# The tile of the rests moved to second to last, and the last unit's stores joined: linear attention feeding a four-expert mixture on one core

## The chip, the core and the metric

The kernel runs on one core of a Trainium2 chip. The core has a matrix engine (TensorE; PE for its matmuls and PEld for its weight loads in the profile), a vector engine (VectorE, DVE), a scalar engine (ScalarE, ACT), a general engine (GpSimd, POOL) and a queue engine (SyncE, SP), and 16 DMA engines that all queues share. Each engine works through its own instructions strictly in the order in which they were emitted, and waits for the others through semaphores. The metric is the device time of one launch in microseconds; lower is better.

## What is computed

```python
# q, k, v: (8 batches, 8 heads, 576 rows, 64); N = 8*576 = 4608, D = 512, E = 4, F = 1024
phi = lambda x: where(x > 0, x, exp(x) - 1) + 1
kv  = einsum('bhsd,bhse->bhde', phi(k), v)                       # 64 x 64 for each head
z   = phi(k).sum(over rows)
x   = (phi(q) @ kv) / (phi(q) . z + 1e-6)                        # attention, per head
x   = x.transpose(0, 2, 1, 3).reshape(4608, 512)                 # one row per token
p   = domain_probs / (domain_probs.sum(-1) + 1e-9)
out = sum over e of p[:, e] * (relu(x @ w1[e]) @ w2[e])          # w1: 512x1024, w2: 1024x512
```

Every batch has 576 tokens: 512 that make a full tile, and a rest of 64.

## The kernel before, in words

**Tiles and units.** The expert part works on nine tiles of 512 tokens. Tiles 0 to 7 are the first 512 tokens of each batch. Tile 8 collects the rests of all eight batches, 8 x 64 tokens; its input is the tensor `xT_left`. A *unit* is one tile with one expert. Each unit has a first layer of two blocks (class `Block`, matmuls of L868, steps p1 to p7 with c22, into the PSUM banks `b` and `e`) and a second layer of 14 products (`layer2_product`, matmuls of L810, into the bank `py`). Both layers use a seven-product scheme of 2 x 2 blocks (Strassen-Winograd), for which GpSimd forms the sums of hidden blocks (`hidden_sum`, L777 to L783) and of tokens (`token_sum`, L849). The output of a tile is kept in four SBUF tiles `acc` (128 tokens x 512 each). For expert 0 ScalarE writes them first (L704), afterwards VectorE adds to them (L706). `acc` has five buffers, so that a new tile's `acc` waits for stores of the tile before.

**Attention ahead of the experts.** While the units of tile j run, the attention of batch j+1 is worked out in between (`batch_steps`). For the full tile of a batch SP issues a transposing DMA of phi(q) (`dma_qT`, L393), PE multiplies (`nd`, L472), VectorE divides, and SP issues four transposing DMAs into `xT` (`dma_xT`, L524). The rest of a batch goes a similar way in smaller pieces: `load_left` (L297) loads k, v and q of the 64 rows as two DMAs each, one for each half of the heads; `left_act` and `left_dve` (L375 to L386) make phi(q) in `qlp`; `dma_qTl` (L401) turns it by two transposing DMAs into `qz`; `nd_left` (L490) is four small matmuls that read `qz`, two VectorE instructions, and two transposing DMAs (L504) into `xT_left`. `qz` is one buffer for all batches. The rest of batch 0 is only begun late: in `before` its q is loaded and turned while tile 7 runs.

**The order of work** is a list. Every step is put at a position, the list is sorted by position, and each engine's instructions are emitted in that order; a step that issues on several engines takes its place on each of them. One unit takes 14 positions, one tile 56. Position 0 of a *window* is the first step of its tile's first unit; window j is that of tile j (units of tile j are `2 * NSLOT * n` positions after `base`). A block that starts at position s has p1 at s, p2 at s+3, p6 at s+5, p7 at s+8, p5 at s+9, p4 at s+11 and p3 at s+13; a unit's second layer starts 20 positions after the unit, at the offsets `L2AT`. `ATTN[1]` holds the positions of a batch's attention within a window, `LATE` those of batch 0's rest. The first part of the kernel, up to the start of tile 2, follows a list written out by hand (`EARLY`); the change does not touch it.

**The end.** The very last unit (tile 8, expert 3) uses another order of products (1, 2, 5, 6, 7, 3, 4), and each quarter of the output (128 tokens x 256 columns) is stored as soon as it is complete. `store` (L693) sends it as two DMAs of 64 KB, one for each batch whose rests lie in it, on two of the queues of SP, ACT and POOL:

```python
by = {(7, 0): "PP", (7, 1): "PA"}.get((p, i), "SA")
store(j, ns, ds, [on[x] for x in by])
```

The full tiles are stored by one DMA of 256 KB for each 128 tokens (L687, SP).

Of the kernel before, what the change touches and what calls it, by code (L numbers as in the profile page):

```python
# [11 lines left out]
FP32 = mybir.dt.float32  # L12
# [18 lines left out]
            v=(18.1, 19.16, 22.55, 30.55),  # L31
            k=(-5.5, 26.3, 27.5, 28.5),
            kd=(0.5, 27.07, 30.0, 30.7),
            lv=23.45,
            lk=15.35,
            lkd=16.3,
            kv=34.0,
            q=(36.4, 36.95, 40.2, 43.4),
            qd=(37.75, 39.0, 40.55, 44.7),
            lq=54.05,  # L40
            lqd=54.5,
            qt=(42.1, 45.0, 45.8, 46.25),
            nd=(46.7, 47.0, 47.05, 47.8),
            xt=(48.15, 50.45, 51.45, 54.8),
            qtl=57.23,
            nl=71.0,
# [4 lines left out]
            v=(4.4, 8.7, 12.1, 14.8),  # L51
            k=(0.3, 2.9, 6.7, 11.25),
            kd=(7.1, 3.84, 14.3, 14.8),
            lv=10.36,
            lk=9.9,
            lkd=11.6,
            kv=19.1,
            q=(20.1, 22.1, 27.0, 30.0),
            qd=(21.75, 27.2, 30.2, 32.3),
            lq=33.9,  # L60
            lqd=38.3,
            qT=35.9,
            nd=(39.3, 40.4, 42.0, 43.5, 45.3, 46.1),
            nl=52.1,
        ),
    ),
    "HSUM": ((-5.2, -3.9, -3.7, -1.3), (0.3, 2.7, 2.7, 5.7)),
    "L2ORD": (2, 5, 1, 6, 3, 7, 4),
# [1 line left out]
    "TSUM": (-6.7, -4.7, -1.6, -0.7),  # L70
    "TSUM1": (3.76, 4.1, 6.3, 9.92),
    "PR": (-21.88, 47.0, 56.27, 39.85),
    "LATE": (4.0, 14.0, 16.0, 24.0),
    "LQ": 'SSSA',
    "LK": 'ASSS',
    "LV": 'SSSS',
# [4 lines left out]
    "KC": ('AA', 'AV', 'VA', 'AA'),  # L81
    "XT": ('AA', 'AA', 'AV', 'AV'),
    "CUT": (((0, 2, 4),) * 4, ((0, 2, 4),) * 4),
    "MOVE": {"m83.10": 512.0, "m83.11": 512.0, "m83.20": 512.0, "m83.21": 512.0, "m82.41": 528.0},
    "WARM": (14, 3, 2, 1, 5),
    "BANK": {'qT0': 'py', 'qT1': 'b', 'nd00': 'py', 'nd00+': 'b', 'kv2': 'py', 'xT00': 'b', 'kv3': 'b', 'nd10+': 'b', 'L00': 'b', 'L10': 'py', 'nd01': 'b', 'xT01': 'py', 'nd11+': 'b', 'L20': 'e', 'L30': 'e', 'L01': 'e', 'L11': 'py', 'L21': 'py', 'L31': 'b', 'b1.qT3': 'py', 'b1.nd30': 'py', 'b1.nd21': 'b', 'b1.q1': 'b', 'b1.qT1': 'py', 'b1.nd01': 'py', 'b1.xT2': 'b', 'b1.nd11': 'py', 'b1.xT0': 'b'},
    "EARLY": (
# [36 lines left out]
def kernel(  # L124
# [10 lines left out]
    nc = tc.nc  # L135
    ATTN, HSUM, L2ORD, L2AT = (CFG[x] for x in ("ATTN", "HSUM", "L2ORD", "L2AT"))

    B, H, S, D = q.shape
    N, E = moe_domain_probs.shape
    _, Dm, F = moe_w1.shape  # L140

    P = 128
    HP = P // 2
# [12 lines left out]
    NACC = 5  # L156
# [3 lines left out]
    NH = NT // 2  # L160
    FH = FC // 2
    DH = Dm // 2
    SE = (0, 1, 2, 3)
    BIG = 3.0e38
    ENG = mybir.EngineType

# [112 lines left out]
    class Batch:  # L279
# [5 lines left out]
            self.vl = vl  # L285

        def alloc_left(self):
            self.rl = praw.tile([P, 3, HG, D], FP32, tag="rawl", bufs=1, name="rl")

        def load_left(self, *names, eng=nc.sync, us=(0, 1)):  # L290
            b = self.b
            if self.rl is None:
                self.alloc_left()
            for i, (name, src) in enumerate((("k", k), ("v", v), ("q", q))):
                for u in us:
                    if name in names:
                        eng.dma_start(  # L297
                            out=self.rl[u * HP : (u + 1) * HP, i],
                            in_=src[b, u * HG : (u + 1) * HG, SM:S].rearrange(
                                "h r d -> r h d"  # L300
                            ),
                        )
# [59 lines left out]
        def left_act(self, *names):  # L362

            for name in names:
                i = ("k", "v", "q").index(name)
                src = self.rl[:, i].rearrange("p h d -> p (h d)")
                parts = []
                for u in range(2) if name == "k" else ():
                    us = slice(u * HP, (u + 1) * HP)
                    parts.append((us, self.kl[us, 2 * u : 2 * u + 2].rearrange("p a d -> p (a d)")))  # L370
                if name == "q":
                    self.ql = pa.tile([P, HG, D], FP16, tag="qlp", bufs=1, name="qlp")
                    parts.append((slice(0, P), self.ql.rearrange("p h d -> p (h d)")))
                for us, dst in parts:
                    nc.scalar.activation(dst, src[us], AF.Identity, bias=1.0)  # L375
                el = aps([P, HG * D], FP32, "psum_el")
                nc.scalar.activation(el, src, AF.Exp)
                self.ph["l" + name] = el, parts
# [302 lines left out]
    def new_py():  # L681
        return ppm.tile([P, Dm], FP32, tag="py", bufs=2, name="py")

    def store(j, ns, cols=slice(0, Dm), engs=(nc.sync, nc.scalar)):
        acc = accs[j, ns][:, cols]
        if j < B:
            nc.sync.dma_start(  # L687
                out=out_b[j, 0:SM].rearrange("(p c) d -> c p d", c=CM)[ns],
                in_=acc,
            )  # L690
        else:
            for u in range(2):
                engs[u].dma_start(  # L693
                    out=out_b[2 * ns + u, SM:S, cols],
                    in_=acc[u * HP : (u + 1) * HP],
                )
# [88 lines left out]
    def layer2_product(j, e, hT, hss, p, i):  # L785


        if (j, e) == (NTILES - 1, E - 1):
            if p == 1:
                pys[j, e, i] = [ppm.tile([P, DH], FP32, tag=tag, bufs=2, name=f"p{tag}") for tag in ("b", "e")]  # L790
            run, side = pys[j, e, i]
        else:
            if p == 2:
                pys[j, e, i] = new_py()
            run, side = pys[j, e, i][:, 0:DH], pys[j, e, i][:, DH:Dm]
        ts = slice(i * P, (i + 1) * P)
        ts2 = slice(NH + i * P, NH + (i + 1) * P)
        w, tw = w2_sb[e], t2_sb[e]
        lo, hi = slice(0, FH), slice(FH, FC)
        ps, lhsT, rhs, first = {  # L800
            1: (run, lambda k: hT[k // 2][:, k % 2, 0, ts], w[:, lo, 0:DH], (j, e) == (NTILES - 1, E - 1)),
            2: (side, lambda k: hT[k // 2][:, k % 2, 1, ts], w[:, hi, 0:DH], True),
            5: (side, lambda k: hss[k // 2][0][:, k % 2, ts], tw[:, 0], True),
            6: (run, lambda k: hss[k // 2][1][:, k % 2, ts], tw[:, 1], False),
            7: (run, lambda k: hT[k // 2][:, k % 2, 0, ts2], w[:, lo, DH:Dm], False),
            3: (side, lambda k: hss[k // 2][3][:, k % 2, ts], w[:, hi, DH:Dm], False),
            4: (run, lambda k: hT[k // 2][:, k % 2, 1, ts2], tw[:, 2], False),
        }[p]
        for k in range(FH):
            nc.tensor.matmul(  # L810
                out=ps,
                lhsT=lhsT(k),
                rhs=rhs[:, k],
                start=first and k == 0,
                stop=k == FH - 1,
                skip_group_check=True,
            )
        yield
        c1, c2 = slice(0, DH), slice(DH, Dm)
        ns, ds, first = {  # L820
            2: (i, c1, True),
            5: (2 + i, c2, True),
            1: (i, c1, False),
            6: (i, c2, True),
            7: (2 + i, c2, False),
            3: (i, c2, False),
            4: (2 + i, c1, True),
        }[p]
        add_acc(j, e, ns, ps, ds, first and e == 0)
        if (j, e) == (NTILES - 1, E - 1):  # L830
            if p in (2, 3, 4, 7):
                yield
                by = {(7, 0): "PP", (7, 1): "PA"}.get((p, i), "SA")
                store(j, ns, ds, [on[x] for x in by])
        elif e == E - 1 and p in (3, 4):
            yield
            store(j, ns)
# [96 lines left out]
    def batch_steps(bt, nxt, put, at, at_next):  # L934
# [50 lines left out]
        else:  # L985
            put(at["qT"], f"b{b}.qT", bt.dma_qT)
            for i in range(6):
                put(at["nd"][i], f"b{b}.nd{i}", numerators, 3 * i, min(3, NPAIR * CM - 3 * i))
        put(at["nl"], f"b{b}.nl", bt.nd_left)
        if first:  # L990
            put(at["xl"], f"b{b}.xl", bt.pe_xl)

# [11 lines left out]
    with tc.manual_schedule(  # L1004
# [53 lines left out]
                put_at(CFG["WS1"][e][i], f"s{e}.{i}", weight_sums, e, i)  # L1058
                put_at(CFG["WS2"][e][i], f"t{e}.{i}", weight_sums2, e, i)
        base = CFG["BLK"][6]  # L1060
        units = [(j, e) for j in range(1, NTILES) for e in range(E)]
        for n, (j, e) in enumerate(units):
            h, hss = [None, None], [[None] * 4, [None] * 4]
            at = base + 2 * NSLOT * n
# [16 lines left out]
        for j in range(0, NTILES - 1):  # L1081
            at = base + 2 * NSLOT * E * (j - 1) if j else 0.0

            def put(pos, *g, at=at):
                put_at(at + pos, *g)

            if j + 1 < B:
                nxt = bts[j + 2] if j + 2 < B else None
                batch_steps(bts[j + 1], nxt, put, ATTN[j > 0], ATTN[1])
            else:  # L1090
                put(CFG["LATE"][0], "b0.alloc", b0.alloc_left)
                put(CFG["LATE"][0], "b0.load", b0.load_left, "q")
                put(CFG["LATE"][1], "b0.lq", b0.left_act, "q")
                put(CFG["LATE"][2], "b0.lqm", b0.left_dve, "q")
                put(CFG["LATE"][2] + 1, "b0.qTl", b0.dma_qTl)
                put(CFG["LATE"][3], "b0.nl", b0.nd_left)
            for i in range(4):
                if j:
                    put(2 * NSLOT * E + CFG["TSUM"][i], f"ts{j + 1}.{i}", token_sum, j + 1, i)
                else:  # L1100
                    put(base + CFG["TSUM1"][i], f"ts1.{i}", token_sum, 1, i)
        work = [(CFG["MOVE"].get(w[2], w[0]), *w[1:]) for w in work]
# [48 lines left out]
```

## Time and profile before

| | |
|---|---|
| runs before, us | 487.11, 487.05, 485.85; median 487.05 |
| span of the profiled execution, first to last instruction, us | 484.6 |
| median of the runs less that span, us | 2.5 |
| PE busy | 474.4 us, 98% of the span |
| DVE, POOL, ACT busy | 377.3, 358.3 and 332.2 us |
| DMA, mean rate over the span | 111 GB/s |

The profile page and the runs do not say which of the three runs the profiled execution is closest to; its span is used beside the median, with the 2.5 us between them kept as they are. In the lines below, a row of the timeline has the start, the length, the engine, the source line, the operation, what it writes and reads, and how many instructions were merged in it. `SPq` and `ACTq` are the queue sides of those engines: the length of a DMA there is the time that the queue takes to issue it, not the time until the data has landed. `L504` is line 504 of the kernel.

### The profile page before, as it was taken

To read this page: it belongs to the slowest core of one execution; us is meant where nothing else is said; L and a number is where in the kernel's file an instruction comes from. 1 tells how busy PE (TensorE), PEld (TensorE's weight loads), DVE (VectorE), ACT (ScalarE), POOL (GpSimd) and SP (SyncE) were. 2 spreads that over 40 slices of the span, in tenths; PEclk is the share of its full clock that TensorE was granted. 3 is DMA by queue.
4 is the path that set the end of the run, shared out by engine and by line. 5 is a ranking of instruction groups with operands and counts; after the bars stand their busy time and mean duration, and the time that the engine had idled before them with its cause. 6 is when DMAs were issued, how large, how long until landed. Compare 5 with 4: busy or idle time off the path is not lost.

```text
span 484.6 us, 12013 instructions
## 1 busy us (share of the span) xinstructions
PE 474.4 (98%) x4565; PEld 407.2 (84%) x4565; DVE 377.3 (78%) x794; ACT 332.2 (69%) x662; POOL 358.3 (74%) x343
## 2 busy tenths in 40 slices
PE   6999999999999999999999999999999999999996
PEld 2766766898889888998889888988898888888885
DVE  5768987987868895888679886988687756775676
ACT  5689989956895599649884888478944565446530
POOL 5566044689966986789777977697769877987775
PEclk9999999999999999999999999999999999999999
DMA  8999987543445154523552446323221020002003
GB/s 293 216 217 254 233 204 201 134 109 88 123 144 111 42 156 150 120 53 115 172 135 56 114 133 157 77 77 106 69 59 28 7 93 2 1 0 89 2 1 87
DMA packets 79945, 53.67 MB, mean 111 GB/s; under 512 B 45152, under 2 KB 72608, under 8 KB 79888
## 3 DMA queue, kind: packets, MB, share of 16 engines
q1 hardware_dynamic: 69760, 40.43, 30.4%
q0 software_dynamic: 8896, 11.47, 12.3%
q10 hardware_dynamic: 1232, 1.02, 0.6%
q8 instruction: 35, 0.57, 0.5%
q14 instruction: 22, 0.18, 0.1%
HBM read 45.16 MB, written 9.44 MB: 113 GB/s over the span
## 4 chain that ended last, share of the span: by engine, by line
PE 90%; DMA 5%; DVE 2%; ACT 2%; issue 0%; POOL 0%; SPq 0%; ACTq 0%; DVEq 0%
PE py L810 38%; PE pb L868 24%; PE pe L868 18%; PE py L715 4%; DMA w<-in_moe_w_dram 2%; PE ph L655 1%; PE psum_nd L472 1%; DMA rawq<-in_q_dram 1%; DMA rawb<-in_q_dram 1%; DMA out_dram<-acc 1%; PE psum_kv L444 1%; PE pb L810 1%; PE pe L810 1%; DVE acc L706 0%; PE psum_nl L490 0%
## 5 line engine op out<-in xcount | busy, mean ns | idle before, releaser
L706 DVE SCALAR_TENSOR_TENSOR acc<-py,p_sb,acc 128x256 f32<-128x256 f32 (+1 forms) x382 | 182.2, 488 | 42.7 <-PE py L810 39.1
L852 DVE CUSTOM_DVE_ANT_0 h<-pe,u 128x512 f16<-128x512 f32 x140 | 96.1, 688 | 45.3 <-PE pe L868 28.0
L868 PEld LDWEIGHTS <-w 128*128 128x128 f16 x1120 | 108.9, 98 | 16.2
L777 POOL TENSOR_TENSOR hs<-h 128x512 f16<-128x512 f16 x64 | 74.7, 1167 | 56.9 <-DVE h L852 51.0
L810 PEld LDWEIGHTS <-h 128*128 128x128 f16 x1024 | 99.6, 98 | 12.2 <-issue 0.9
L810 PE MATMUL py<-w,h 128*128 128x256 f16 x744 | 106.4, 273 | 0.5 <-ACT acc L704 0.5
L879 ACT COPY u<-pb 128x512 f32<-128x512 f32 x140 | 82.4, 591 | 29.7 <-PE pb L868 27.8
L779 POOL TENSOR_TENSOR hs<-hs,h 128x512 f16<-128x512 f16 x64 | 74.1, 1157 | 26.8 <-PE py L810 24.3
L868 PEld LDWEIGHTS <-s 128*128 128x128 f16 x840 | 81.2, 98 | 12.6 <-DVE s L747 0.7
L868 PE MATMUL pb<-tt,w 128*128 128x256 f16 x560 | 83.8, 273 | 0.0
L810 PEld LDWEIGHTS <-hs 128*128 128x128 f16 x768 | 74.4, 98 | 8.8 <-issue 0.2
L783 POOL TENSOR_TENSOR hs<-h,hs 128x512 f16<-128x512 f16 x64 | 74.2, 1159 | 0.8 <-POOL h L781 0.5
L781 POOL TENSOR_TENSOR h<-h 128x512 f16<-128x512 f16 x64 | 74.6, 1165 | 0.1
L810 PE MATMUL py<-t,hs 128*128 128x256 f16 x496 | 74.1, 273 | 0.0
L901 ACT ACTIVATE h<-pe 128x512 f16<-128x512 f32 x70 | 41.9, 599 | 41.1 <-PE pe L868 40.5
L894 ACT COPY pe<-pb 128x512 f32<-128x512 f32 x70 | 40.0, 571 | 41.3 <-PE pb L868 15.8
L922 ACT ACTIVATE h<-pb 128x512 f16<-128x512 f32 x70 | 41.8, 599 | 6.3 <-PE pb L868 6.2
L868 PE MATMUL pb<-tt,s 128*128 128x256 f16 x280 | 41.9, 273 | 0.2 <-DVE s L747 0.2
L868 PE MATMUL pe<-tt,s 128*128 128x256 f16 x280 | 42.0, 273 | 0.0
L868 PE MATMUL pe<-xT,s 128*128 128x256 f16 x248 | 37.1, 273 | 0.0
L868 PE MATMUL pb<-xT,w 128*128 128x256 f16 x248 | 37.1, 273 | 0.0
L868 PE MATMUL pe<-xT,w 128*128 128x256 f16 x248 | 37.0, 273 | 0.0
(133 smaller groups left out, 594.6 us busy)
## 6 DMA issues: line engine op xcount, KB each, us to landing
out_dram<-acc SPq DMA_DIRECT2D x32, 256.0 KB, 2.5
w<-in_moe_w_dram POOLq DMA_DIRECT2D x14, 512.0 KB, 10.6
rawb<-in_k_dram SPq DMA_DIRECT2D x24, 256.0 KB, 3.1
rawb<-in_q_dram SPq DMA_DIRECT2D x24, 256.0 KB, 2.7
rawb<-in_v_dram SPq DMA_DIRECT2D x24, 256.0 KB, 2.8
w<-in_moe_w_dram POOLq DMA_DIRECT2D x4, 256.0 KB, 5.8
rawb<-in_k_dram POOLq DMA_DIRECT2D x4, 256.0 KB, 10.5
rl<-in_q_dram SPq DMA_DIRECT2D x16, 64.0 KB, 3.1
```

The source lines that it names most:

```text
L706: nc.vector.scalar_tensor_tensor(out=acc, in0=ps, scalar=pscal, in1=acc, op0=AO.mult, op1=AO.add)
L777: nc.gpsimd.tensor_tensor(out=hs[0], in0=a21, in1=a22, op=AO.add)
L779: nc.gpsimd.tensor_tensor(out=hs[1], in0=hs[0], in1=a11, op=AO.subtract)
L781: nc.gpsimd.tensor_tensor(out=a21, in0=a11, in1=a21, op=AO.subtract)
L783: nc.gpsimd.tensor_tensor(out=hs[3], in0=a12, in1=hs[1], op=AO.subtract)
L810: nc.tensor.matmul(out=ps, lhsT=lhsT(k), rhs=rhs[:, k], start=first and k == 0, stop=k == FH - 1, skip_group_check=True,)
L852: nc.vector._custom_dve(TENSOR_ADD_SAT, out=out, in0=ps, in1=u, s0=BIG, s1=0.0)
L868: nc.tensor.matmul(out=ps[:, kk], lhsT=lk(kc), rhs=rhs[:, kc], start=first and kk == 0 and kc == 0, stop=kc == 1, skip_group_check=True,)
L879: nc.scalar.copy(u, self.b)
L894: nc.scalar.copy(self.e5, self.b)
L901: nc.scalar.activation(self.h[:, :, 0, 0:NH], self.e5, AF.Relu)
L922: nc.scalar.activation(self.h[:, :, 1, 0:NH], self.b, AF.Relu)
```

## The change

Five things change.

1. **Order of tiles.** Units run over tiles 0 to 6, then 8, then 7 (`TILES`). The last unit is now tile 7 with expert 3 (`LAST`), and the token sums follow the same order.
2. **Stores.** The last unit's quarters go out by one DMA of 128 KB each, on SP for i = 0 and on ACT for i = 1; POOL issues none. Tile 8, now in the middle of the stream, is stored by two DMAs of 128 KB for each 128 tokens, all on SP.
3. **Batch 0's rest** is worked out in window 3 (while tile 3 runs and the attention of batch 4 is made) instead of window 7: its q is loaded at position 36, phi on ACT at 48.6 and on DVE at 50, the two transposing DMAs of L401 at 50.1, and `nd_left` at 55.4. Before, in window 7, these were 4, 14, 16, 17 and 24. Its raw q goes into a buffer of `acc` instead of a buffer of its own.
4. **Batch 4's rest**: `nd_left` moves from position 52.1 to 47.2 of the same window 3.
5. **Batch 7's rest** (window 6): phi(q) from 33.9 (ACT) and 38.3 (DVE) to 23.3 and 24.4, and with it its transposing DMAs from 40.3 to 26.4; `nd_left` from 52.1 to 37.2.

```diff
+        dict(
...
+            lq=23.3,
+            lqd=24.4,
...
+            nl=37.2,
+        ),
...
-    "LATE": (4.0, 14.0, 16.0, 24.0),
+    "LATE": (36.0, 48.6, 50.0, 50.1, 55.4),
...
+    TILES = (*range(B - 1), NTILES - 1, B - 1)
+    LAST = (TILES[-1], E - 1)
...
         def alloc_left(self):
-            self.rl = praw.tile([P, 3, HG, D], FP32, tag="rawl", bufs=1, name="rl")
+            if self.b:
+                self.rl = praw.tile([P, 3, HG, D], FP32, tag="rawl", bufs=1, name="rl")
+            else:
+                self.rl = pm.tile([P, 2, HG, D], FP32, tag="acc", bufs=NACC, name="rl")
...
-    def store(j, ns, cols=slice(0, Dm), engs=(nc.sync, nc.scalar)):
+    def store(j, ns, cols=slice(0, Dm), eng=nc.sync):
         acc = accs[j, ns][:, cols]
         if j < B:
-            nc.sync.dma_start(
-                out=out_b[j, 0:SM].rearrange("(p c) d -> c p d", c=CM)[ns],
+            eng.dma_start(
+                out=out_b[j, 0:SM].rearrange("(p c) d -> c p d", c=CM)[ns][:, cols],
                 in_=acc,
             )
         else:
             for u in range(2):
-                engs[u].dma_start(
+                eng.dma_start(
                     out=out_b[2 * ns + u, SM:S, cols],
                     in_=acc[u * HP : (u + 1) * HP],
                 )
...
-        if (j, e) == (NTILES - 1, E - 1):
+        if (j, e) == LAST:
             if p in (2, 3, 4, 7):
                 yield
-                by = {(7, 0): "PP", (7, 1): "PA"}.get((p, i), "SA")
-                store(j, ns, ds, [on[x] for x in by])
+                store(j, ns, ds, (nc.sync, nc.scalar)[i])
...
-        put(at["nl"], f"b{b}.nl", bt.nd_left)
+        put(at["nl"] - 4.9 * (b == 4), f"b{b}.nl", bt.nd_left)
...
-        units = [(j, e) for j in range(1, NTILES) for e in range(E)]
+        units = [(j, e) for j in TILES[1:] for e in range(E)]
...
-                batch_steps(bts[j + 1], nxt, put, ATTN[j > 0], ATTN[1])
-            else:
+                batch_steps(bts[j + 1], nxt, put, ATTN[(j > 0) + (nxt is None)], ATTN[1])
+            if j == 3:
                 put(CFG["LATE"][0], "b0.alloc", b0.alloc_left)
                 put(CFG["LATE"][0], "b0.load", b0.load_left, "q")
                 put(CFG["LATE"][1], "b0.lq", b0.left_act, "q")
                 put(CFG["LATE"][2], "b0.lqm", b0.left_dve, "q")
-                put(CFG["LATE"][2] + 1, "b0.qTl", b0.dma_qTl)
-                put(CFG["LATE"][3], "b0.nl", b0.nd_left)
+                put(CFG["LATE"][3], "b0.qTl", b0.dma_qTl)
+                put(CFG["LATE"][4], "b0.nl", b0.nd_left)
...
-                    put(2 * NSLOT * E + CFG["TSUM"][i], f"ts{j + 1}.{i}", token_sum, j + 1, i)
+                    put(2 * NSLOT * E + CFG["TSUM"][i], f"ts{TILES[j + 1]}.{i}", token_sum, TILES[j + 1], i)
```

In the diff, five steps of the last two units that an entry of `MOVE` sets to a fixed position keep their positions under the names of tile 7.

More of the change, by code (lines that the diff above doesn't have):

```diff
@@ L65 @@
         ),
+        dict(
+            v=(4.4, 8.7, 12.1, 14.8),
+            k=(0.3, 2.9, 6.7, 11.25),
+            kd=(7.1, 3.84, 14.3, 14.8),
+            lv=10.36,
+            lk=9.9,
+            lkd=11.6,
+            kv=19.1,
+            q=(20.1, 22.1, 27.0, 30.0),
+            qd=(21.75, 27.2, 30.2, 32.3),
+            lq=23.3,
+            lqd=24.4,
+            qT=35.9,
+            nd=(39.3, 40.4, 42.0, 43.5, 45.3, 46.1),
+            nl=37.2,
+        ),
     ),
@@ L83 @@
     "CUT": (((0, 2, 4),) * 4, ((0, 2, 4),) * 4),
-    "MOVE": {"m83.10": 512.0, "m83.11": 512.0, "m83.20": 512.0, "m83.21": 512.0, "m82.41": 528.0},
+    "MOVE": {"m73.10": 512.0, "m73.11": 512.0, "m73.20": 512.0, "m73.21": 512.0, "m72.41": 528.0},
     "WARM": (14, 3, 2, 1, 5),
@@ L162 @@
     DH = Dm // 2
-    SE = (0, 1, 2, 3)
+    TILES = (*range(B - 1), NTILES - 1, B - 1)
+    LAST = (TILES[-1], E - 1)
     BIG = 3.0e38
@@ L297, in load_left @@
                         eng.dma_start(
-                            out=self.rl[u * HP : (u + 1) * HP, i],
+                            out=self.rl[u * HP : (u + 1) * HP, i if self.b else 0],
                             in_=src[b, u * HG : (u + 1) * HG, SM:S].rearrange(
@@ L365, in left_act @@
                 i = ("k", "v", "q").index(name)
-                src = self.rl[:, i].rearrange("p h d -> p (h d)")
+                src = self.rl[:, i if self.b else 0].rearrange("p h d -> p (h d)")
                 parts = []
@@ L800, in layer2_product @@
         ps, lhsT, rhs, first = {
-            1: (run, lambda k: hT[k // 2][:, k % 2, 0, ts], w[:, lo, 0:DH], (j, e) == (NTILES - 1, E - 1)),
+            1: (run, lambda k: hT[k // 2][:, k % 2, 0, ts], w[:, lo, 0:DH], (j, e) == LAST),
             2: (side, lambda k: hT[k // 2][:, k % 2, 1, ts], w[:, hi, 0:DH], True),
@@ L829, in layer2_product @@
         add_acc(j, e, ns, ps, ds, first and e == 0)
-        if (j, e) == (NTILES - 1, E - 1):
+        if (j, e) == LAST:
             if p in (2, 3, 4, 7):
                 yield
-                by = {(7, 0): "PP", (7, 1): "PA"}.get((p, i), "SA")
-                store(j, ns, ds, [on[x] for x in by])
+                store(j, ns, ds, (nc.sync, nc.scalar)[i])
         elif e == E - 1 and p in (3, 4):
```

## The prediction

> **What bounds the kernel now.** I read the engine totals first, then the busy time of the windows, the timeline of SP, PE and ACT at the places that the change touches, and the last microseconds.
>
> ```profile
> PE 474.4 (98%) x4565; PEld 407.2 (84%) x4565; DVE 377.3 (78%) x794; ACT 332.2 (69%) x662; POOL 358.3 (74%) x343
> 165.80:216.70 50.90, 50.90 (x511) 45.58 (x509) 41.05 (x91) 37.92 (x76) 40.74 (x38) 1.00 0.45 115
> 369.60:418.60 49.00, 49.00 (x453) 43.95 (x452) 33.36 (x68) 26.64 (x50) 40.35 (x37) 1.00 0.09 29
> 467.50:484.60 17.10, 12.52 (x114) 10.82 (x111) 12.46 (x28) 1.18 (x2) 10.67 (x11) 0.94 0.22 61
> ```
>
> The last three rows are windows (start:end, length, then busy time of PE, PEld, DVE, ACT, POOL, granted clock, DMA share, GB/s): window 3, window 7, and the end. In windows 3 and 7 PE is busy for all of their length. So no step that is moved there can win time for the middle of the kernel; a step can only lose time, by making PE wait. What can be won lies behind PE's last matmul (480.0), in the stores. The first part is unchanged, and the work of PE is the same in number.
>
> **The stores at the end.**
>
> ```profile
> 479.62 0.92 DVE L706 SCALAR_TENSOR_TENSOR acc<-pb,p_sb,acc 128x256 f32<-128x256 f32 x2
> 481.42 0.55 ACTq L693 DMA_DIRECT2D out_dram<-acc  x1
> DMA to landing us min/median/max: 2.2/2.2/2.3
> ```
>
> The last data is ready at 479.62 + 0.92 = 480.54, but its second DMA goes out at 481.42, 0.88 us later, since ACT still issues earlier ones at about 0.65 us apart. (The third row is of the last DMA on SP and the last on ACT.) It lands 2.2 us after, at 483.6; from there to the end of the span it is 1.0 us. With one DMA for each quarter, SP and ACT take turns: VectorE finishes a quarter every 0.45 us, so each queue gets one in 0.9 us, more than its 0.55 us. The queue is free, and the last issue follows the data within 0.05 us, at 480.59: **-0.83 us**. The DMA is now 128 KB instead of 64; the 256 KB stores of L687 land in 2.0 us at best and 2.4 in the median, so I take 2.3 instead of 2.2: **-0.75 us** (from -0.5 to -1.0). PE's and VectorE's order in the last unit is the same for tile 7 as for tile 8.
>
> **Batch 0's rest in window 3.** This is where I expect the loss. SP in that window:
>
> ```profile
> 195.78 2.55 SPq L393 DMA_TRANSPOSE qT<-qp  x1
> 198.42 1.29 SPq L297 DMA_DIRECT2D rl<-in_k_dram  x2
> 199.76 1.27 SPq L297 DMA_DIRECT2D rl<-in_v_dram  x2
> 201.07 2.41 SPq L297 DMA_DIRECT2D rl<-in_q_dram  x2
> 203.60 2.47 SPq L401 DMA_TRANSPOSE qz<-qlp  x2
> 206.23 5.13 SPq L524 DMA_TRANSPOSE xT<-x_sb  x4
> 214.74 2.44 SPq L504 DMA_TRANSPOSE xT_left<-x_sl  x2
> ```
>
> From 195.78 to 211.36 SP issues without a break: one transposing DMA costs it 1.2 us, so the queue, not the DMA engines, is full. The pause before 214.74 is the wait for batch 4's `nd_left` (PE at 213.62). By position the changed queue reads: L393 (35.9), **two loads for batch 0 (36)**, six loads (39.3), two L401 (40.3), four L524 (40.4 to 46.1), two L504 of batch 4 (now 47.2), **two L401 of batch 0 (50.1)**, two L504 of batch 0 (55.4).
>
> - The two new loads: such a pair takes 1.27 to 1.29 us, the third pair 2.41. Six loads took 5.18, 0.86 each, so two cost 1.3 to 2.4; I take 0.86 x 2 = 1.7. The four L524 then end at 211.36 + 1.7 = 213.06.
> - Batch 4's L504 no longer wait for PE, they wait for SP: 213.1 to 215.55 (2.44).
> - Batch 0's first L401 goes out at 215.6, the second 1.29 later (203.60 to 204.89) at 216.9, and lands 2.3 us after, at **219.2**.
>
> PE needs both. What stands there:
>
> ```profile
> 216.03 0.60 PE L868 MATMUL pe<-xT,s 128*128 128x256 f16 x4
> 216.47 0.60 PE L810 MATMUL py<-w,h 128*128 128x256 f16 x4
> 216.91 0.60 PE L868 MATMUL pb<-xT,w 128*128 128x256 f16 x4
> ```
>
> These are positions 55 (p3 of a block at 42), 55.2 (a second-layer product at 48 + 7.2) and 56 (p1 of the next tile). `nd_left` at 55.4 falls between the last two, so it is due at 216.9. PE is in order: everything behind it waits to 219.2, **+2.3 us**. With loads of 1.3 it is 1.9, with 2.4 it is 3.0; and were the loads to cost nothing, 0.6 would stay. PE has no slack later in which to win it back. The four matmuls themselves are only moved from window 7.
>
> What else belongs to this step: phi(q) is two ACT and one DVE instruction of about 0.45 us each. At 48.6 ACT has a pause of 1.1 us (209.6 to 210.7), and DVE reaches 50 at about 211.5, well ahead of SP: nothing. The buffer of `acc`: four are held by tile 3, the fifth is free, and it is back before tile 4 asks: nothing, or up to 0.3 if the buffers come round in another order and ACT waits for a store, as it does at 293.27, where PE lost 0.2 us. SP's loads for batch 5 come 3 us later at most, behind the two L504 of batch 0, while PE has stood still for 2.3: nothing. GpSimd's token sums for tile 4 need the L524, 1.7 later; the second sum starts at 215.2, the last L524 lands at 214.2: nothing.
>
> **Batch 4 earlier.** `nd_left` at 47.2 comes after the group at 208.82, at 209.26. The second L401 of batch 4 now lands at 207.2 + 1.7 = 208.9. It fits by 0.35 us; with the slowest loads it is late by 0.3, but then the later stall is shorter by that. So 0.
>
> **Batch 7 earlier.** Its phi(q) at 23.3 falls into the busiest stretch of ACT:
>
> ```profile
> 340.35 0.61 ACT L347 ACTIVATE psum_ee<-rawb 128x512 f32<-128x512 f32 x1
> 340.97 0.47 ACT L704 ACTIVATE acc<-py,p_sb 128x256 f32<-128x256 f32 x1
> 342.08 0.60 PE L810 MATMUL py<-t,hs 128*128 128x256 f16 x4
> ```
>
> Two ACT instructions of about 0.43 us come between the first two rows. ACT is without a pause from 338 to 345.6, so the first `acc` ends at 342.3 instead of 341.44, and the PE group of 342.08, which overwrites that half of `py`, waits some 0.3 us: **+0.3** (0 if ACT catches up first, 0.86 at most, what is put in).
>
> **Tile 8 in the middle.** Its stores are eight DMAs on SP instead of four. The third pair ends its issue some 0.65 us later and lands at about 442.4, and ACT's fourth `acc` of the next tile begins at 442.81: 0, at most 0.2.
>
> **The sum.** -0.75 + 2.3 + 0.3 = +1.85 on the span, 484.6 to 486.4. The span lies 2.5 under the median of the runs, which I keep: 487.05 + 1.85 = **488.9 us**. Its own range is 487.8 (-1.0 + 1.9 - 0.15 for small gains in the last unit) to 490.0 (-0.5 + 2.6 + 0.86, loads near their middle).
>
> **Rivals.**
>
> *A: the clock falls in the stall (490.7).* The granted clock drops soon after PE stops:
>
> ```profile
> 482.00:482.50 0.50, 0.00 (x0) 0.00 (x0) 0.00 (x0) 0.00 (x0) 0.00 (x0) 0.99 0.96 303
> 482.50:483.00 0.50, 0.00 (x0) 0.00 (x0) 0.00 (x0) 0.00 (x0) 0.00 (x0) 0.50 0.75 240
> 1.19 4.66 PE L997 MATMUL warm_ps<-qz 128*128 128x512 f16 x13 [1.19 <-DVE qz L176]
> ```
>
> It is at half by 482.5, 2.5 us after the last matmul, and a stall of 2.3 is near that. What half rate costs: the first 13 matmuls of 512 columns take 4.66 us, where at full rate a 256-column one starts every 0.109 us, so 13 of double length would take 2.8. That is 1.8 us lost, hence 488.9 + 1.8 = 490.7. Against it: one stop of the clock at the end is all that the trace shows, and 2.3 is shorter than 2.5. The Trainium skill ("TensorE: Matmul & The Clock Gate", section "What's actually happening") has the clock halved only after a whole free-running window of about 3.4 us without work. By that rule a stall of 2.3 can't halve it, and the sum stays at 488.9. The trace does not quite agree, with its 2.5 us. I give this case 0.13.
>
> *B: the loads hide (487.2).* If the two loads cost SP nothing, because the third pair's 2.41 us was a wait that comes anyway, the second L401 lands at 217.5 and PE loses 0.6. With +0.3 for batch 7 and -0.75 this is +0.15: no change. It decides at SP's shift: with 1.3 us or less the whole change stays under 0.3%. The profile speaks against it, as the other two pairs were issued back to back at 1.3. I give 0.17.
>
> *C: PE does not stall (486.3).* If batch 0's L401 land before 216.9, the end's -0.75 is all that is left: 486.3, not slower. This needs SP to reach position 50.1 by 213.3 instead of 215.6, that is, to issue the eight transposing DMAs ahead of it from 205.3 on at 1.0 us each, gaps included. Those of this window take 1.2 and more, and 1.3 from one to the next. 0.06.
>
> **Chances.** Forecast 0.64, A 0.13, B 0.17, C 0.06. About 0.3% (1.5 us) is what a measurement of this kernel can tell from no change; the three runs of before are 1.3 us apart. Slower by more than that is over 488.5: seven tenths of the forecast and all of A, 0.58. Within: the rest of the forecast, B and C, 0.38. Faster by over 0.3% would need more than the end can give: 0.04. The range of 486.9 to 490.8 leaves out C, the tails of the forecast and part of A.
>
> **What would show it.** In the changed profile: SP back to back from 195.8 to about 218; PE idle of about 2.3 us at 217, put down to L490 and the DMA into `qz`, and none at batch 4's `nd_left`; a gap of PE of 0.3 us near 344.5 at batch 7's phi(q); the last store issued within 0.1 us of the last DVE instruction. The prediction is wrong if PE runs through window 3, or if the clock column falls below 1.00 there.

## The result and the profile after

The changed kernel took **488.41 us** in the median of 7 runs (486.74 to 490.56), beside 487.05 for 7 runs of the kernel before (485.85 to 487.36). The ratio is 1.0046, with a 95% interval of 1.003 to 1.0062: 2.2 us slower by the ratio, 1.4 by the medians. Line numbers are about 20 higher than before: L830 is the second layer, L887 the first, L510 `nd_left`, L421 the transposing DMAs into `qz`, L524 those into `xT_left`, L544 those into `xT`, L317 the loads of a rest, L707 the last unit's stores.

The profiled execution is the slowest of the seven (490.56). Its span is 488.8, 4.2 over that of before, and it holds one loss that not every run has. First the engine totals of the page, then one row of the waits (us in all, times, the longest):

```profile
PE 476.9 (98%) x4565; PEld 408.3 (84%) x4565; DVE 378.6 (77%) x794; ACT 331.6 (68%) x662; POOL 356.3 (73%) x340
```

```profile
PE psum_nl L510 <- DMA qz<-qlp: 2.5, 2, 1.5
```

PE has as many instructions as before (4565) and is busy 2.5 us longer, so its instructions became longer somewhere; and it waits 2.5 us, in two pieces, for the DMAs of L421. The timeline of PE (start, length, engine, line, operation, number merged, idle time before and what ended it) has both:

```profile
216.98 0.60 PE L830 MATMUL py<-w,h 128*128 128x256 f16 x4
219.04 0.23 PE L510 MATMUL psum_nl<-kvz,qz 128*128 128x130 f16 x1 [1.46 <-DMA qz<-qlp]
220.31 0.34 PE L510 MATMUL psum_nl<-kvz,qz 128*128 128x130 f16 x3 [1.03 <-DMA qz<-qlp]
220.49 0.60 PE L887 MATMUL pb<-xT,w 128*128 128x256 f16 x4
```

Ends of matmuls are modelled, so I count from start to start. The group of 216.98 would be followed at 217.42 (four times 0.109). The next block starts at 220.49, and the four small matmuls take 0.23 when nothing holds them up. So 220.49 - 217.42 - 0.23 = **2.84 us** are lost. The same stretch in windows, cut where the granted clock changes (columns as in the prediction):

```profile
217.68:221.09 3.41, 1.01 (x10) 0.82 (x11) 0.95 (x4) 0.00 (x0) 3.41 (x5) 1.00 0.11 22
221.09:224.50 3.41, 3.41 (x18) 2.44 (x17) 1.21 (x3) 3.21 (x6) 0.79 (x1) 0.50 0.11 22
224.50:228.00 3.50, 3.50 (x34) 3.12 (x33) 3.00 (x6) 2.51 (x6) 3.13 (x3) 1.00 0.50 150
```

The stall fills most of the first row and ends at 220.3, but in the second row the clock stands at 0.50: PE is "busy" all of it and gets 18 matmuls done, where the third row has 34. From start to start, the 20 matmuls from 220.93 up to the group of 224.78 take 3.85 us; at 0.109 each they would take 2.18, so another **1.7 us** are lost. SP's side of the window:

```profile
201.71 2.07 SPq L317 DMA_DIRECT2D rl<-in_v_dram  x2
...
207.85 5.12 SPq L544 DMA_TRANSPOSE xT<-x_sb  x4
213.06 3.54 SPq L524 DMA_TRANSPOSE xT_left<-x_sl  x2
216.72 2.44 SPq L421 DMA_TRANSPOSE qz<-qlp  x2
```

The queue is in the order that the prediction wrote down, and back to back from 196.3 to 219.2. Two things differ. Of the four pairs of loads (199.06 to 205.10) only this one, 2.07, is over 1.29: the longer pair comes once, as it did among three before. And the pair of L524 took 3.54, where it had taken 2.44. Last the tail, where the last data is ready at 484.81 + 0.92 = 485.73:

```profile
484.81 0.92 DVE L726 SCALAR_TENSOR_TENSOR acc<-pb,p_sb,acc 128x256 f32<-128x256 f32 x2
...
485.76 0.34 ACTq L707 DMA_DIRECT2D out_dram<-acc  x1
```

The last DMA goes out 0.03 us after its data and lands 1.97 us later. From PE's end to the end of the span it is 3.57 us, against 4.55 before: **-0.98**.

Together: 0.5 by which the unchanged first part happened to run longer (the matmuls of batch 4's `kv` start at 183.63 instead of 183.12), 2.84, 1.7, 0.17 for a longer wait for `acc` at 299 (501 ns from one matmul's start to the next, instead of 335 at 293.79 before), and -0.98. That is 4.2, the whole difference of the spans.

### The profile page after: what moved, and what is told of

Read it like the earlier page. It is cut to its first block, busy times and chain, and to the rows that moved or that the text cites. A ratio compares the mean times of both kernels' runs of the same rounds, so it can differ in the third digit from the quotient of the medians.

```text
span 488.8 us, 12011 instructions
## 1 busy us (share of the span) xinstructions
PE 476.9 (98%) x4565; PEld 408.3 (84%) x4565; DVE 378.6 (77%) x794; ACT 331.6 (68%) x662; POOL 356.3 (73%) x340
## 4 chain that ended last, share of the span: by engine, by line
PE 94%; DMA 2%; DVE 2%; ACT 1%; issue 0%; SPq 0%; ACTq 0%
PE py L830 38%; PE pb L887 25%; PE pe L887 19%; PE py L735 6%; PE ph L675 1%; PE psum_nd L492 1%; PE psum_kv L464 1%; DMA rawq<-in_q_dram 1%; DMA out_dram<-acc 1%; PE pb L830 1%; PE pe L830 1%; DMA qz<-qlp 0%; PE psum_nl L510 0%; DVE acc L726 0%; ACT ee L601 0%; DVE kpos L586 0%
## 5 line engine op out<-in xcount | busy, mean ns | idle before, releaser
L887 PEld LDWEIGHTS <-w 128*128 128x128 f16 x1120 | 109.1, 98 | 16.3
L830 PEld LDWEIGHTS <-h 128*128 128x128 f16 x1024 | 99.7, 98 | 12.6 <-issue 1.2
L830 PE MATMUL py<-w,h 128*128 128x256 f16 x744 | 106.7, 273 | 0.8 <-ACT acc L724 0.8
L887 PEld LDWEIGHTS <-s 128*128 128x128 f16 x840 | 81.5, 98 | 12.3
L887 PE MATMUL pb<-tt,w 128*128 128x256 f16 x560 | 84.3, 274 | 0.0
L830 PEld LDWEIGHTS <-hs 128*128 128x128 f16 x768 | 74.8, 98 | 9.2 <-issue 0.2
L830 PE MATMUL py<-t,hs 128*128 128x256 f16 x496 | 74.7, 274 | 0.0
L887 PE MATMUL pe<-tt,s 128*128 128x256 f16 x280 | 42.5, 275 | 0.0
L887 PE MATMUL pb<-tt,s 128*128 128x256 f16 x280 | 41.8, 273 | 0.0
L887 PE MATMUL pe<-xT,s 128*128 128x256 f16 x248 | 37.1, 273 | 0.0
L887 PE MATMUL pb<-xT,w 128*128 128x256 f16 x248 | 37.1, 273 | 0.0
L887 PE MATMUL pe<-xT,w 128*128 128x256 f16 x248 | 37.0, 273 | 0.0
```

Of the source, the lines that this page charges most:

```text
L830: nc.tensor.matmul(out=ps, lhsT=lhsT(k), rhs=rhs[:, k], start=first and k == 0, stop=k == FH - 1, skip_group_check=True,)
L887: nc.tensor.matmul(out=ps[:, kk], lhsT=lk(kc), rhs=rhs[:, kc], start=first and kk == 0 and kc == 0, stop=kc == 1, skip_group_check=True,)
```

## The experiments

Theory: the loss is batch 0's `nd_left` standing on PE ahead of its data, plus in some runs the half clock that follows. Rivals: the new order of tiles or the stores cost something; or the long L524 belongs to the loads or the changed order on SP. The first four kernels shared one chip (before: 486.84, n 28), the last four another (486.52, n 20). Each is the changed kernel but for the edit shown.

| kernel | runs | median, us | ratio to before | 95% interval | PE lost at `nd_left`, us |
|---|---|---|---|---|---|
| nl_later | 12 | 485.65 | 0.9979 | 0.9966 to 0.9992 | 0.00 |
| load_early | 11 | 489.45 | 1.0046 | 1.0027 to 1.0066 | 2.83 |
| nl_earlier | 5 | 492.02 | 1.0109 | 1.0091 to 1.0128 | 4.85 |
| split_stores | 12 | 487.35 | 1.0014 | 1.0002 to 1.0027 | 0.00 |
| after_again | 8 | 489.53 | 1.0048 | 1.0029 to 1.0066 | 2.79 |
| nl_57 | 12 | 487.03 | 1.0018 | 1.0002 to 1.0033 | 1.41 |
| old_order | 7 | 490.55 | 1.0074 | 1.0048 to 1.0099 | 2.94 |
| pe_pad | 1 | (490.08) | | | 1.69 |

The last column is from each profiled execution, from start to start as above.

### nl_later: batch 0's nd_left at 62.0

```diff
-    "LATE": (36.0, 48.6, 50.0, 50.1, 55.4),
+    "LATE": (36.0, 48.6, 50.0, 50.1, 62.0),
```

> The changed kernel with batch 0's nd_left at position 62 instead of 55.4, nothing else. Theory (PE waits at nd_left for batch 0's second L421, which lands 2.8 us after PE is due, and the half clock after it comes from that stop): no PE idle at L510 in window 3, granted clock 1.00 until after the last matmul in every run, and a time of 486.1 us, 487.05 less 0.95 for the stores. Rival (the loss is in the crowding of window 3 itself, or in the new order of tiles, and nd_left is only where it shows): the idle time moves to another place, and the time stays near 488.4.

Measured: 485.65, a ratio of 0.9979. The four matmuls now run straight through, at their new place:

```profile
222.33 0.60 PE L887 MATMUL pe<-xT,s 128*128 128x256 f16 x4
222.77 0.39 PE L510 MATMUL psum_nl<-kvz,qz 128*128 128x130 f16 x4
223.00 0.60 PE L887 MATMUL pb<-xT,w 128*128 128x256 f16 x4
```

Nothing waits ahead of them, the clock is 1.00 until after the last matmul, and what is left of the change is its gain, 0.45 us more than expected. "In every run" was too much: eleven of the twelve runs have a mean clock of 0.998 or more, one has 0.995 and took 487.63. One number in a list turns a slower kernel into one that is faster than both. This is the main evidence for the theory.

### load_early: the two new loads at position 31

```diff
-    "LATE": (36.0, 48.6, 50.0, 50.1, 55.4),
+    "LATE": (31.0, 48.6, 50.0, 50.1, 55.4),
```

> The changed kernel with batch 0's load of q at position 31 instead of 36, where SP has pauses. Theory: SP's queue behind L413 is shorter by the two loads, 1.1 to 1.3 us, so that the wait at L510 shrinks from 2.8 to about 1.6 us; with so short a stop the clock stays at 1.00 in nearly all runs; 487.3 to 487.7 us. Rival (the second L421 is late because of the transposing DMAs alone, and the two loads are hidden in a pause that comes anyway): the wait stays at 2.8 us, and the time at 488.4.

Measured: 489.45, 1.0046, the same ratio as with the loads at 36. A miss. SP did reach batch 0's L421 2.4 us sooner, but that was worth nothing. Its timeline of SP:

```profile
211.75 2.47 SPq L524 DMA_TRANSPOSE xT_left<-x_sl  x2
214.35 3.46 SPq L421 DMA_TRANSPOSE qz<-qlp  x2
```

L524 now takes its usual 2.47, and the extra microsecond has passed to L421 behind it (3.46). So the long issue belongs to a moment (about 214.3 to 216.5), not to an instruction and not to the loads. The second L421 was issued at 216.63 and landed at 219.70, 3.07 us later instead of 2.3, and PE, due at 216.87, could go on at 219.75. So something else must be at work at that moment; pe_pad, below, is about it.

### nl_earlier: nd_left at 53.0

```diff
-    "LATE": (36.0, 48.6, 50.0, 50.1, 55.4),
+    "LATE": (36.0, 48.6, 50.0, 50.1, 53.0),
```

> The changed kernel with batch 0's nd_left at position 53 instead of 55.4: the same wait begins some 2.4 us earlier and ends at the same moment, so PE stands still for 5.3 us. If the clock halves whenever PE stood still for most of a window of 3.4 us (the changed kernel's record has it after 2.8): half clock in every run, 486.1 + 5.3 + 1.7 = 493.1 us, with little spread. If it takes a whole window of 3.4 us without work, at a random phase: a whole one fits into 5.3 us in about half of the runs, and the runs fall into two groups, 491.4 and 493.1. Rival for the place of the loss: if PE's stop at nd_left were not on the path, the time would not move by 2.4 us or more.

Measured: 492.02 (1.0109), and all five runs between 491.15 and 492.22, at clocks of 0.993 to 0.996. The sign and the clock are as expected, the size is 1.1 under the expected 493.1: 0.45 of it because PE lost 4.85 and not 5.3, another 0.45 because the kernel without the wait took 485.65 (nl_later) and not 486.1. The rest is not assigned. PE is due at 214.70 and has the first half of its data at 218.20 and the second at 219.47. The windows of this kernel:

```profile
213.92:217.33 3.41, 0.94 (x9) 0.59 (x7) 0.93 (x3) 1.19 (x2) 3.41 (x4) 1.00 0.15 31
217.33:220.74 3.41, 1.56 (x9) 1.13 (x10) 0.61 (x2) 0.00 (x0) 2.80 (x4) 0.50 0.06 12
```

The clock is halved from 217.33 on, here for two windows (to 224.16). In the first of them PE hardly has work until 219.77; from there to the end of the second the half clock costs 2.1 us, counted from start to start, of which the second, with 18 matmuls, has about 1.7 as in the changed kernel.

### nl_57: nd_left at 57.1

```diff
-    "LATE": (36.0, 48.6, 50.0, 50.1, 55.4),
+    "LATE": (36.0, 48.6, 50.0, 50.1, 57.1),
```

> The changed kernel with batch 0's nd_left at position 57.1 instead of 55.4, four groups of matmuls (1.75 us) later. Theory: the second L421 still lands at the same moment, so PE waits 2.84 - 1.75 = 1.1 us; that is too short for the clock, which stays at 1.00 in all runs; 485.65 + 1.1 = 486.8 us, with the spread of the kernel before. Rival (the clock halves by the sum of small stops, or the wait does not follow the position): 488 us or more in some runs.

Measured: 487.03 (1.0018). In the profile PE loses 1.41 us and the clock stays at 1.00:

```profile
218.47 0.22 PE L510 MATMUL psum_nl<-kvz,qz 128*128 128x130 f16 x1
219.92 0.34 PE L510 MATMUL psum_nl<-kvz,qz 128*128 128x130 f16 x3 [1.24 <-DMA qz<-qlp]
```

The wait is 0.3 longer than expected, as the second L421 landed 2.85 us after its issue instead of 2.3. Nine of the twelve runs show clocks of 0.999 or 1.000; three show 0.996 and took 488.39 to 489.23, where the theory had 1.00 in all runs and the rival 488 or more in some. They do not decide: of the 20 runs of the kernel before on this chip, which has no such stall, three are at 0.994 to 0.996 too (487.76 to 488.66), and the mean clock does not tell the place.

With nl_later, nl_57, the changed kernel and nl_earlier there are four lengths of the stall: 0, 1.41, 2.8 and 4.85. As us of 487 by the ratios they stand at -1.0, +0.9, +2.3 and +5.3, that is 1.9, 3.3 and 6.3 above nl_later. The time follows the stall, with 0.5 to 1.5 more than its length.

### after_again: the changed kernel beside the last three

No edit.

> The changed kernel once more, for more runs beside the others. Theory: the wait at L510 is 2.8 us in every run; where its phase fits a window of 3.4 us the clock halves and costs 1.7 us more. The runs fall into two groups, about 488.3 and 490.2 us, with some half of the runs in each (three of the first seven are over 489.5). Rival (one cause with a spread): a single group around 488.5.

Measured: 489.53, 1.0048; on another chip the ratio is nearly that of the first measurement (1.0046). The two groups of equal size did not come: six of the eight runs have mean clocks of 0.996 or 0.997 and took 489.12 to 490.31; the other two (0.999 and 1.000) took 487.61 and 488.91, so that the groups almost touch. The profiled execution has the same stall (2.79) and the same half clock behind it, for 3413 ns from 220.15, and a fetch, of which more below, with a single L524 of 2.44.

### old_order: the rests moved alone, tiles 0 to 8 and the stores as before

```diff
-    TILES = (*range(B - 1), NTILES - 1, B - 1)
+    TILES = tuple(range(NTILES))
...
-                store(j, ns, ds, (nc.sync, nc.scalar)[i])
+                by = {(7, 0): "PP", (7, 1): "PA"}.get((p, i), "SA")
+                for u in range(2):
+                    on[by[u]].dma_start(
...
```

The five entries of `MOVE` get back their names of tile 8.

> The moved rests alone: the changed kernel, but with the tiles in the old order (0 to 8) and the last unit's stores as in the kernel before. Theory: the same wait of 2.8 us at L510 and the same half clock in about half of the runs, and the old end: 486.84 + 2.84 = 489.7 us without and 491.4 with the half clock, median about 490.4. Rival (the new order of tiles costs something of its own, which the end hides): under 489.5.

Measured: 490.55 (1.0074), with a stall of 2.94 and a half clock behind it; the profiled execution, the slowest of the seven (492.3), has one more half clock at 12.81, in the part that no edit touches. So the whole loss belongs to the moved rest, and the order of tiles with the joined stores only takes some of it back: 490.55 - 489.53 = 1.0 in medians of the same chip, though these two intervals overlap.

### split_stores: nl_later with the last unit's stores in halves, on the old three queues

```diff
-                store(j, ns, ds, (nc.sync, nc.scalar)[i])
+                by = {(7, 0): "PP", (7, 1): "PA"}.get((p, i), "SA")
+                for u in range(2):
+                    us = slice(u * HP, (u + 1) * HP)
+                    on[by[u]].dma_start(
+                        out=out_b[j, 0:SM].rearrange("(p c) d -> c p d", c=CM)[ns][us, ds],
+                        in_=accs[j, ns][us, ds],
+                    )
```

> As nl_later (nd_left at 62), but the last unit's quarters go out by two DMAs of 64 KB on the queues that the kernel before used (SP and ACT; POOL and POOL; POOL and ACT). Theory: the last issue comes 0.8 us after the last data instead of at once, and each issue takes 0.55 us instead of 0.34: 0.8 to 1.0 us slower than nl_later, 487.0 us. Rival (the joined stores save nothing that lands last, and the shorter end comes from tile 7's other rows in memory): the same time as nl_later.

Measured: 487.35 against nl_later's 485.65, on the same chip, in 12 runs each: 1.7 us, more than expected. Their intervals (1.0002 to 1.0027 and 0.9966 to 0.9992) do not touch. ACT's issues in the last unit and the landings, split first, then joined (min/median/max of one issue in ns, first and last start):

```profile
L856 ACTq DMA_DIRECT2D out_dram<-acc x3: 557/562/604, 479.4 to 480.8; - x3
...
DMA to landing us min/median/max: 2.5/2.8/3.2
```

```profile
L707 ACTq DMA_DIRECT2D out_dram<-acc x3: 338/339/351, 479.4 to 481.1; - x3
...
DMA to landing us min/median/max: 1.9/2.0/2.2
```

Joined stores are fewer, and each issue is also 0.2 us shorter and each landing 0.6 to 1.0 us sooner. From PE's end to the end of the span it is 5.09 split and 3.54 joined. The Trainium skill ("DMA: Bandwidth & Descriptors", section "Rules for kernel authors") says not to bother with two transfers to disjoint halves of the partitions and to use one of 128 partitions. The runs agree, and add a price: 1.7 us, here where it stands on the end. That price includes the third queue, since POOL issues in the split form alone, and it is more than the change itself gained: the kernel before and old_order, which store tile 8's rows in halves, take 4.55 and 4.65 from PE's end to the end of the span, so about half a microsecond of the 5.09 goes with the rows of tile 7. The rows of tile 7 made the split end longer, not shorter as the rival had it.

### pe_pad: PE's instruction stream shifted

The record of DMA transfers shows a third party: beside nearly every issue of SP that is long for its kind, a transfer of 16 KB of kind "instruction" runs on one DMA engine (beside 102 of the 116 issues in the ten profiles that took over 0.3 us more than the median of their line and tile). This is the changed kernel from 214.8 to 216.3 (kind: packets, MB, share of the DMA engines; the last line has the issue's landing time):

```profile
q8 instruction: 1, 0.02, 5.7%
...
xT_left<-x_sl SPq DMA_TRANSPOSE x1, 3.4
```

It starts at 214.85 and takes 1.36 us. Such fetches come 9 to 18 us apart, and the page counts 35 of them; over PE's 4565 matmuls that is one for each 130 with their weight loads. If it is PE's instruction stream that is fetched, then 96 tiny matmuls ahead of the real work, in place of 8 of the 14 warm-up ones, must move the fetches, and the long issue with them.

```diff
-        for i in range(n):
+        for i in range(6 if n == 14 else n):
...
+        for i in range(96 if n == 14 else 0):
+            nc.tensor.matmul(
+                out=warm_ps[:, 0:2], lhsT=qz[:, 0, 0], rhs=qz[:, 0, 0, 0:2], start=True, stop=True
+            )
```

> The changed kernel with the first 14 warm-up matmuls (512 columns) replaced by 6 of them and 96 of 2 columns, at the start, where PE has nothing else to do; no result changes. It adds 88 matmuls to PE's stream and so shifts the moments at which PE's next 16 KB of instructions are fetched (every 128 matmuls, 13.3 us) by 88 matmuls, to about 206 and 219 us in place of 201.5 and 214.9. Theory (a transposing DMA that meets such a fetch takes SP 2.3 us instead of 1.2, and one did so at 214.3 in the changed kernel): no long issue between the fourth L544 and the second L421 of batch 0, and a wait at L510 of 1.7 to 1.9 us instead of 2.84. Rival (the long issue comes from something at that place in SP's own queue): it stays there, and the wait stays at 2.8. The time says nothing, since the start is changed.

Measured: in this stretch the fetches now start at 208.88 and 223.32 instead of 201.49 and 214.85. Both are later than the expected 206 and 219, but the kernel as a whole runs 2.7 us later here (batch 4's `kv` starts at 186.34 instead of 183.63). The long issue moved along, to batch 4's L421 (3.13 for the two), and L524 is back at 2.47:

```profile
207.15 3.13 SPq L421 DMA_TRANSPOSE qz<-qlp  x2
...
215.67 2.47 SPq L524 DMA_TRANSPOSE xT_left<-x_sl  x2
```

So the long issue does not belong to its place in SP's queue. In all there are 36 fetches instead of 35, for the 88 more matmuls. PE's wait is shorter:

```profile
220.58 0.23 PE L510 MATMUL psum_nl<-kvz,qz 128*128 128x130 f16 x1 [0.30 <-DMA qz<-qlp]
221.86 0.34 PE L510 MATMUL psum_nl<-kvz,qz 128*128 128x130 f16 x3 [1.05 <-DMA qz<-qlp]
```

Its loss at `nd_left` fell from 2.84 to 1.69, as expected if the fetch was behind it; the clock did not fall there. The one time of 490.08 says nothing, since the padding costs time of its own and the clock was halved for a window at 88.7.

## Why the prediction was right, and where it was not

- **What bounds the kernel**: right. The middle could only lose time, and lost it where PE was made to wait. nl_later, in which PE does not wait there, has the gain alone.
- **Stores, -0.75**: right in kind and a little small. It measured -0.98 in the profile, and nl_later, in which PE loses nothing at `nd_left`, is 1.0 us faster than the kernel before by its ratio (0.4 to 1.7). The issue after the data was as worked out (0.03 us late). I had put in 0.1 for a slower landing of the bigger DMA; it landed in 2.0 instead of 2.2.
- **Loads on SP, +1.7**: too large. Seven of the eight issues take 0.61 to 0.63 each, and a long one (1.41) comes once, as it did before (1.75); the extra 1.1 in the third pair's 2.41 was a wait that comes anyway, a fetch at 201.05. So the price is about 1.1 to 1.3, and in this the reason of rival B was right.
- **L524 at 2.44**: the step that failed on the other side. It took 3.54, since the fetch fell into it; before, the fetch of 214.01 had fallen into SP's pause ahead of the same two DMAs (L504 there). The two errors nearly cancel: with 1.1 and 1.1 the second L421 was issued at 217.99 and landed at 220.26, 2.84 past the due time where 2.3 was forecast.
- **Batch 7, +0.3**: zero in the changed kernel's profile. ACT's two instructions start at 346.29 and 346.59; then come, in the timeline of ACT and of PE:

```profile
346.90 0.47 ACT L724 ACTIVATE acc<-py,p_sb 128x256 f32<-128x256 f32 x1
...
347.49 0.60 PE L830 MATMUL py<-t,hs 128*128 128x256 f16 x4
```

  Against its PE group the first `acc` is 0.51 later than before (1.15 instead of 0.64 behind it), not 0.86. It ends at 347.37, and the matmuls that overwrite `py` start at 347.49, on time. PE did lose time in this window in after_again (0.34) and in nl_57 (0.76), but not to phi(q): in nl_57 ACT had been idle for 0.80 us ahead of the `acc` of 346.22 that PE waited for, and a store of the tile before landed at 346.11; in after_again the idle time is 0.38, the `acc` at 349.36 and the landing at 349.25. By these times it is the same wait for a buffer of `acc` as at 299 in the changed kernel.
- **Batch 4 and tile 8, 0**: right; PE waits at no other L510, and nothing waits for tile 8's stores.
- **Rival A, the half clock**: I gave it 0.13, with 1.8 us; it measured 1.7, and it comes far more often. Both profiled executions of the changed kernel have it at this place, and so has old_order's. Of load_early's eleven runs, five at mean clocks of 0.998 or more took 487.1 to 488.1 us, and six at 0.993 to 0.997 took 489.45 to 491.57; its profiled execution is one of the five, with the same stall and no half clock. Of the changed kernel's fifteen runs eleven are under 0.998. So after a stall of 2.8 the half clock comes in half of the runs or more, and the chance of 0.13 was far too small. Where the mean clock alone is known, as in most runs, the place is not shown: of the 20 runs of the kernel before on the second chip five are under 0.998 as well.
- **The sum**: forecast +1.85; the runs give +1.36 in medians and +2.2 by the ratio. It came out by errors that offset each other: loads -0.6, the fetch +1.1, batch 7 -0.3, stores -0.23, the wait for `acc` +0.17. That is +2.0 by the profile, and about 0.8 more with a half clock of 1.7 in half of the runs. The 2.8 is above both measures, but within the interval of the ratio (1.5 to 3.0 us). That the forecast of 488.9 came so near the measured 488.41 is in part luck, then: the wait at `nd_left` was foreseen, its size came right by two errors, and the half clock was left out of the sum. The mechanism could be read from the profile of before, its single terms only to about half a microsecond.

What stays open: how the second L421 of load_early came to take 3.07 us to land, so that its data came no sooner. The fetch of 214.32 was over by then (215.50), but the traces have a second kind of instruction transfer, of 8 KB on another queue. Two of them fall just ahead of this landing, from 218.44 and from 218.88 (load_early, 218.4 to 218.9):

```profile
q14 instruction: 2, 0.02, 10.7%
```

The ten profiles hold 140 transposing DMAs into `qz`. In 22 of them such a transfer starts 1.3 to 2.0 us after the issue, and these landed after 2.85 to 3.38 us; nl_57's second one (217.03, after 2.85) is among them. The 90 that no instruction transfer of either kind met landed after 2.27 to 2.38. No run moves the 8 KB transfers, so this is a regular coincidence, not a cause shown.

## What to carry to other kernels

When a step is moved on an in-order engine, compare the time at which its place comes up with the time at which its data lands, instruction by instruction on the feeding queue: 2.8 us of difference cost more than the whole gain here, and 6.6 positions later cost nothing. Ask after each stall what it does to the clock, since a stall of a length near the clock's window costs half a window more in some runs and not in others, and the spread of the times shows it. At the end of this kernel, one store for each finished piece on alternating queues was worth more than splitting each over several queues.

## What the runs showed of the hardware

**Instruction fetches meet DMA issues.** In the ten profiles a 16 KB fetch takes 0.9 to 1.95 us on one DMA engine. The 21 transposing DMAs into `qz`, `xT` and `xT_left` in whose first 0.75 us a fetch began took SP 1.46 to 2.44 us to issue instead of 1.2; later in a fetch many were issued in 1.16 as usual. Of the loads of a rest after 115 us, those issued between 0.1 us before and 0.4 us after a fetch began took 0.93 to 1.75 instead of 0.61. The fetches follow the count of PE's instructions: 88 more of these moved the fetches and the long issue. In the kernel before the same fetches are there, at 201.05 under the third pair of loads, whose 2.41 us the prediction read as something of the loads.

**The clock halves after windows that are not empty.** The changes of the granted clock are 3413 ns apart or a multiple of it. It was halved after windows with PE busy for 0.94 us (nl_earlier), 1.01 (the changed kernel) and 0.94 (old_order) of 3.41, also at the end of the kernel before (0.95 from 479.07 to 482.48, the drop that the prediction read as 2.5 us of standing still), and after 1.30 (pe_pad, 85.29 to 88.70); it was not after 1.57 (the end of nl_57, 480.26 to 483.68), 1.68 (load_early, 218.02 to 221.43) or 2.17 (nl_57, 217.44 to 220.85). It came back after one busy window. One case does not fit: old_order's clock was halved at 12.81 after a window with 1.94 us, while windows of the first part with 1.73 to 1.98 in other runs were not followed by it. So busy time as the profile counts it orders the cases near the stall, but is not the whole rule. The Trainium skill ("TensorE: Matmul & The Clock Gate", section "What's actually happening") has it fall after an idle window of about 3.4 us. The length agrees; but the window need not be idle, under a third busy was enough. So a stall of 2.8 us is caught or not by where it falls in the window: in the changed kernel it leaves 1.01 us of work in one window, in load_early 1.68.
